# Reordering the first units of an attention-then-MLP kernel: loads, pads, copies, a table load, zero matmuls and one filler

## The chip, the cores and the metric

The kernel runs on one core of a Trainium2 chip. The metric is device time in microseconds (us), the median of several executions; less is better. The engines named here are TensorE (PE; its weight loads are shown as PEld), VectorE (DVE), ScalarE (ACT), GpSimd (POOL) and SyncE (SP), which here does nothing but issue DMAs. ScalarE and GpSimd issue some DMAs too. Each engine runs its own instructions strictly in the order in which the program gives them, and waits on semaphores for what it needs from the others.

## What is computed

A linear attention with a decaying state, followed by a two-layer MLP with SiLU:

```python
B, H, S, D = 4, 8, 768, 48                  # batch, heads, sequence, head size
for t in range(S):                          # r, k, v: (B, H, S, D); w, u: (H, D)
    cur = einsum('bhd,bhe->bhde', u * k[t], v[t])
    y[t] = einsum('bhd,bhde->bhe', r[t], state + cur)
    state = w[..., None] * state + einsum('bhd,bhe->bhde', k[t], v[t])
x = y.transpose(0, 2, 1, 3).reshape(3072, 384)
h = x @ w_in                                # 384 x 2048
out = (h * sigmoid(h)) @ w_out              # 2048 x 384
```

## The kernel before

**Units.** The sequence is cut into six chunks of 128 steps. A unit is one chunk of one batch (all eight heads): unit `i` is chunk `i // 4` of batch `i % 4`, 24 units in all. A unit's r, k and v are three loads of 192 KB each into `rin`, `kin` and `vin` (eight buffers each), in rows of 48 floats in slots of 64; `pad` (line 169, VectorE) or `pad_copy` (line 173, ScalarE) zeroes the 16 spare columns of r and k.

**One unit of chunk 0.** In the words of the order list below: `T` turns r and k into PSUM by TensorE transposes (line 272); `rT` and `kT` multiply them by powers of the decay on VectorE (line 289); `P` forms the products within the chunk on TensorE (line 380); `n` masks them on VectorE (line 386); `V` multiplies by v on TensorE (line 396); `e` adds the bonus term and evicts to `y` on VectorE (line 401); `yT` transposes y on TensorE (line 591), and `xT` or `xTD` copies the result to `xT`, on ScalarE or on VectorE (`copy_x`, lines 593 to 595). Beside it GpSimd makes the bonus: `ku` (line 240), `ru` (line 245) and, after a row sum `rd` on VectorE (line 253), `vu` (line 258). It also makes the decayed k, `kc` (line 248), which `S` on TensorE (line 419) multiplies with v into the new state. `v16` casts v to 16 bits on ScalarE (line 263). Units 4 and up work on halves of a chunk, with `Q` (line 478), `D` (line 455) and `Z` (lines 544, 552 and 561) in the place of `S`, `P` and `V`.

**The MLP.** `L` is a group of six to twelve matmuls of the first layer into PSUM (`hps`, line 606), `G` its SiLU on ScalarE into `gT` (line 615). The second layer accumulates 16 matmuls per 128 tokens (`ops`, line 628). Both are cut into pieces; a piece of the second layer is four matmuls of 128x384. Pieces wait in a list of fillers, and `fill(n)` issues the next `n` of them, so that TensorE has work while the attention waits on other engines.

**The order.** The schedule is written out by hand. Up to the first half of chunk 1 the order is a list of words (lines 717 to 731) that the loop at line 732 turns into instructions, on whichever engine the step belongs to; `lr`, `lk` and `lv` are loads that SyncE issues, `ak` is a load of k that ScalarE issues, `pd` and `pa` are the two kinds of pads, `tab` loads ScalarE's table for SiLU (line 227; before it ScalarE has the table for Ln and Exp), `clear` and `spin` are matmuls on zeros that no one reads (lines 186 and 181), `i_q` and `i_o` are loads of `w_in` and `w_out` that GpSimd issues, `ub` and `uc` (lines 205 and 208) spread u over the partitions as `u_bc`, which `ru` reads. After the list, the loop at line 748 handles two units per turn, from unit 6 on. In its turn for units 6 and 7 it issues, for TensorE: `sums(6)`, `product_halves(6)`, `fill(4)` at line 782, `outputs_halves(6)`, the transposes `turn(8)` and `turn(9)` (r, then k, of each), and then `fill(4)` at line 801 and more fillers before `sums(8)`.

Of the kernel before, what the change touches and what calls it, by code (L numbers as in the profile page):

```python
# [16 lines left out]
def kernel(  # L17
# [11 lines left out]
    nc = tc.nc  # L29

    B, H, S, D = r.shape
# [19 lines left out]
    def unit(i):  # L51
        return divmod(i, B)
# [52 lines left out]
    idle = cst.tile([128, 512], F16)  # L105
# [53 lines left out]
    lamC = cst.tile([128, H, D], FP)  # L159
    lamH = cst.tile([128, H, D], FP)  # L160
# [4 lines left out]
    lamN = cst.tile([128, H, D], FP)  # L165
# [9 lines left out]
            nc.scalar.copy(out=dst[i][:, :, D:64],  # L175
                           in_=idle[:, 0:128].rearrange("p (h d) -> p h d", h=H))

    def spin(n):
        zs = ps.tile([128, 512], FP, name="zs", tag="moe", bufs=4)
        for _ in range(n):  # L180
            nc.tensor.matmul(zs, idle[:, 0:128], idle, start=True, stop=True)

    def clear():
        for t in att:
# [18 lines left out]
    def spread_row(name, src):  # L203
        spread[name] = ps.tile([128, HD], FP, name="bc", tag="moe", bufs=4)
        nc.tensor.matmul(spread[name], ones, src, start=True, stop=True)
# [28 lines left out]
    def bonus_products(i):  # L234
        bonus_ku(i)
        bonus_rku(i)
# [60 lines left out]
    def by_planes(i):  # L297
        return i > 2 * B + 1
# [193 lines left out]
    def state_first(i):  # L492
        s1 = L(i)["s1"] = wrk.tile([PR, 2, NP, D], FP, name="s1")
        if unit(i)[0]:
            nc.vector.tensor_tensor(out=s1, in0=summed(i, 0), in1=L(i)["sdec"], op=ALU.add)  # L495
        else:
            nc.vector.tensor_copy(out=s1, in_=summed(i, 0))
        if early(i):
            spread_pairs(nc.scalar.copy, inner_pairs[i // 2 % 2], s1)
            return  # L500
        for j in range(2):
            spread_state(nc.scalar.copy, j, inner[i // 2 % 2], s1)
# [115 lines left out]
    def l1(sc, b0, nb, ft):  # L618
        l1_mm(sc, b0, nb, ft)
        l1_silu(sc, b0, nb, ft)  # L620
# [47 lines left out]
    def fill(n):  # L668
        for _ in range(n):
            if fillers:  # L670
                fillers.pop(0)()
# [14 lines left out]
    halved = [lambda ft=ft: l1(1, 0, 2, ft) for ft in range(0, NFT, 2)]  # L686

    def piece(word, f):
        b0, ft = word.split(".")
        f(0, *blocks[b0], int(ft))  # L690
# [6 lines left out]
        "wy": lambda: columns(nc.scalar, wpT, w, 0), "lnw": powers_r, "eK": exponents_k,  # L697
        "lamK": powers_k, "uc": copy_u, "wb": lambda: spread_row("w", w_row),
        "ub": lambda: spread_row("u", u_row), "lnwb": ln_w, "lamC": powers_c, "lamH": powers_h, "lamN": powers_n,
        "tab": silu_table, "clear": clear, "spin": lambda: None, "H": lambda: halved.pop(0)(),  # L700
    }
    unit_steps = {
        "T": turn, "rT": lambda i: decay_one(i, 0), "kT": lambda i: decay_one(i, 1),
# [12 lines left out]
    }  # L716
    order = """
        ur kz0 id itr lr0 wy pd0 ak0 cz2 kz3 itc wr mk wx cz1 mh lnw eK cg3 lamK kz4 kz1 lk1
        id16 lr1 pd3 lr3 lk3 clear 6*spin lv0 cg0 lv1 kz7 lr2 ak2 ku0 lv3 lr5 kz2 lv2 ub pd1 lv4
        lr4 lk4 lv5 pd2 lk5 lk7 lr6 lk6 uc T0 1*spin T1 lr7 lv7 kT0 pa4 rT0 ru0 ku1  # L720
        v160 pd5 lv6 rT1 kz6 rd0 kT1 wb ru1 P0 n0 2*spin rd1 P1 vu0 lnwb T2 n1 v161 2*spin
        pd7 lamC lamH lamN pa6 i_q0 V0 v162 tab rT2 e0 kT2 ku2 T3 1*spin yT0 V1 kz5 vu1 i_q1 ru2
        xTD0 e1 P2 yT1 kT3 rd2 rT3 ku3 xTD1 P3 ru3 n2 rd3 v163 n3 L0.0 vu2 kc0 1*spin G0.0
        vu3 V2 L0.2 V3 G0.2 L0.4 e2 i_q2 e3 kc1 yT2 yT3 S0 G0.4 xT2 xTD3 kc2 L0.6 L2.4 G0.6
        st0 L2.0 scA0 v164 kc3 L2.6 ku4 i_q3 v165 L2.2 T4 rT4 kT4 G2.4 ru4 G2.2 T5 G2.0 G2.6
        L4.8 G4.8 L4.10 kT5 G4.10 L4.9 kc4 ku5 S2 L4.11 rd4 rT5 st2 sc2 kc5 sd4 ru5 G4.9
        G4.11 rA4 vu4 i_o0 Q4 D4 rA5 s1_4 ku7 L4.12 rd5 vu5 m4 s2_4 G4.12 L4.13 G4.13 T6 Z4
        L4.14 G4.14 L4.15 z4 yT4 2*spin yT5 i_o2 i_o1 ku6 xT4 xT5 rT6 T7 G4.15 rT7 v167 sd6
        kT6 v166 ru6 lr8 kc6 kc7 H H rd6 i_o3 H vu6 lr9 rP7 rA6 sn4 H H lk8 lk9 sx4 lv9 lv8
        ru7 kT7  # L730
    """
    for word in order.split():
        if "*" in word:
            n, word = word.split("*")
            spin(int(n))
        if word in steps:
            steps[word]()
        elif word[0] == "L":
            piece(word[1:], l1_mm)
        elif word[0] == "G":  # L740
            piece(word[1:], l1_silu)
        else:
            unit_steps[word[:-1]](int(word[-1]))
# [4 lines left out]
    for i in range(B + 2, NU, 2):  # L748
        sc, b = unit(i)
        nxt = range(i + 2, min(i + 4, NU))  # L750
        after = range(i + 4, min(i + 6, NU))
        split = i + 2 < NU and by_planes(i + 2)
        sums(i)
        product_halves(i)
        state_first(i)
        masked_halves(i)
        state_second(i)
        if by_planes(i + 4) and not by_planes(i):
            rescale_state(i)
        if i == B + 2:  # L760
            bonus_sum(i + 1)
            bonus_v(i + 1)
        if i == 2 * B:
            for n in nxt:
                split_k(n, nc.scalar.copy)
        if split:
            turn_planes()
        if b and split:
            for n in nxt:
                cast_k(n)  # L770
                cast_v(n)
        for n in nxt:
            bonus_products(n)
            if not split:
                decayed_k(n)
        if i > B + 2 or sc < NCH - 1:
            next_state(i)
        if not b and split:
            for n in nxt:
                cast_k(n, nc.gpsimd.tensor_copy)  # L780
                cast_v(n, nc.gpsimd.tensor_copy)
        fill(3 if b and split else 4)
        outputs_halves(i)
        next_crossed(i)
        for n in nxt:
            turn(n)
        evict_halves(i)
        turn_y_dma(i)
        if b:
            fillers.extend((first(sc) if sc > 1 else rest_first(sc)) + second(sc))  # L790
        for n in nxt:
            if split:
                decay_one(n, 0)
                if b:
                    join_k(n)
            else:
                decay(n)
        for dst, src in ((kin, k), (rin, r), (vin, v)):
            for n in after:
                ld(n, dst, src)  # L800
        fill(4)
        if i > 2 * B and not b and split:
            for n in nxt:
                join_k(n)
        for n in nxt:
            bonus_sum(n)
            if not split:
                cast_v(n)
            bonus_v(n)
        for n in after:  # L810
            weighted_k(n)
        if after and by_planes(i + 4) and not i == B + 2:
            for n in after:
                split_k(n)
        for n in nxt:
            fill(2)
            decay_r16(n, True)
        if i == 2 * B and split:
            for n in nxt:
                join_k(n)  # L820
        fill((5 if b and split else 4) if i < NU - 4 else 2)
# [31 lines left out]
```

## Time and profile before

| | |
|---|---|
| median of 3 executions | 185.11 us (184.15 to 185.25) |
| the profiled execution | 185.49 us, of which the span from its first to its last instruction is 183.8 us |
| TensorE busy | 174.5 us (95% of the span), 2801 matmuls |
| VectorE, ScalarE, GpSimd busy | 117.0, 115.8, 129.3 us |
| DMA queue of SyncE (q1) | 98224 packets, 23.86 MB, 66.5% of 16 engines' time |
| granted TensorE clock | 1.00 over the span |

The span is the time between the first and the last instruction on the core; the rest of the 185.49 us lies around it. In a timeline row the first number is the start in us from the beginning of the span, the second how long the merged group lasted, then engine, line, operation, what it writes and reads, shapes and count; in brackets, how long the engine had been idle and what ended that. A row with SPq, ACTq or POOLq is the issuing of a DMA. A matmul's duration includes the time until its result is out, so that matmuls that overlap are judged by the spacing of their starts. "DMA share" is the time of all packets over the time of 16 engines; it can be somewhat over 1, since packets overlap in an engine.

### The profile page before, as it was taken

The page shows a single profiled execution, that of the slowest core. Times are in us where ns is not written, and L with a number is a line of the kernel's source. Part 1 is how long each engine was busy: PE and PEld are TensorE (multiplying, and loading weights), DVE is VectorE, ACT ScalarE, POOL GpSimd, SP SyncE. Part 2 cuts the span into 40 slices and gives each one's busy share as a digit, 9 for nine tenths or more (in the row PEclk, how much of TensorE's full clock was granted, in tenths as well). Part 3 has the DMA queues.
Part 4 walks back from the last instruction along what each step waited for, and adds up shares of the span by engine and source line. Part 5 has one row for each costly group of instructions (what it writes and reads, how often), then busy time and mean ns, then how long its engine had stood idle before and what let it go on. Part 6 is the DMA issues. An engine that isn't in the chain of part 4 may idle for free.

```text
span 183.8 us, 6611 instructions
## 1 busy us (share of the span) xinstructions
PE 174.5 (95%) x2801; PEld 113.9 (62%) x2801; DVE 117.0 (64%) x231; ACT 115.8 (63%) x208; POOL 129.3 (70%) x179
## 2 busy tenths in 40 slices
PE   7977899999899999999899999999999999999993
PEld 2555786588666976656556555657656566555562
DVE  5999728897977985865775955776944974000120
ACT  4471787699145797398597488797588781299200
POOL 7999999898899979869979769879769700000000
PEclk9999999999999999999999999999999999999999
DMA  5999999899697799999599999499799201410022
GB/s 95 238 192 216 178 175 200 154 224 225 129 189 210 114 202 184 199 183 202 114 178 177 162 209 213 92 183 160 183 197 250 49 4 46 128 43 0 10 79 86
DMA packets 102865, 27.89 MB, mean 152 GB/s; under 512 B 97586, under 2 KB 102324, under 8 KB 102836
## 3 DMA queue, kind: packets, MB, share of 16 engines
q1 hardware_dynamic: 98224, 23.86, 66.5%
q0 software_dynamic: 2176, 3.15, 10.1%
q10 hardware_dynamic: 2436, 0.46, 1.3%
q8 instruction: 22, 0.36, 0.8%
q14 instruction: 7, 0.06, 0.1%
HBM read 20.45 MB, written 4.72 MB: 137 GB/s over the span
## 4 chain that ended last, share of the span: by engine, by line
PE 72%; POOL 17%; DMA 5%; issue 5%; ACT 0%; POOLq 0%
PE ops L628 33%; PE hps L606 26%; DMA kin<-in_k_dram 5%; PE att L455 4%; POOL ku L240 4%; POOL rku_f L245 3%; PE att L272 3%; POOL vu L258 2%; POOL kc L248 2%; PE yp L552 2%; PE sp L478 2%; PE ops L653 1%; PE yp L561 1%; POOL win L84 1%; POOL wout L89 1%
## 5 line engine op out<-in xcount | busy, mean ns | idle before, releaser
L606 PE MATMUL hps<-xT,win 128*128 128x512 f16 (+1 forms) x360 | 66.3, 338 | 0.1
L615 ACT ACTIVATE gT<-hps 128x512 f16<-128x512 f32 x96 | 55.3, 597 | 12.2 <-PE hps L606 8.9
L628 PE MATMUL ops<-wout,gT 128*128 128x384 f16 x368 | 62.9, 326 | 0.1
L606 PEld LDWEIGHTS <-win 128*128 128x128 f16 x360 | 39.0, 114 | 21.1 <-issue 0.4
L628 PEld LDWEIGHTS <-gT 128*128 128x128 f16 x368 | 35.0, 98 | 23.9 <-ACT gT L615 0.8
L401 DVE TENSOR_TENSOR y<-yp,vu 64x384 f16<-64x384 f32 (+1 forms) x34 | 18.9, 555 | 11.3 <-PE yp L561 5.5
L245 POOL TENSOR_TENSOR rku_f<-ku,u_bc 128x384 f32<-128x384 f32 x24 | 24.2, 1010 | 1.4
L240 POOL TENSOR_TENSOR ku<-kin,rin 128x384 f32<-128x384 f32 x24 | 24.2, 1007 | 0.7 <-DMA rin<-in_r_dram 0.6
L258 POOL TENSOR_TENSOR vu<-vin,rku 128x384 f32<-128x384 f32 x24 | 19.6, 828 | 6.8 <-DVE rku L253 6.8
L289 DVE TENSOR_TENSOR rT<-att,lamR 112x512 f16<-112x512 f32 (+1 forms) x26 | 17.8, 684 | 4.2 <-PE att L272 3.8
L326 ACT COPY kT<-blocks 112x1024 uint16<-112x1024 uint16 x14 | 15.6, 1160 | 7.6 <-DMA blocks<-planes 7.5
L634 ACT COPY osb<-ops 128x384 f32<-128x384 f32 x20 | 9.4, 475 | 16.5 <-PE ops L628 12.5
L495 DVE TENSOR_TENSOR s<-sp,sdec 112x384 f32<-112x384 f32 x10 | 5.6, 557 | 16.0 <-PE sp L478 15.4
L636 DVE COPY osb<-ops 128x384 f32<-128x384 f32 x3 | 1.7, 557 | 21.3 <-PE ops L628 21.3
L462 DVE TENSOR_TENSOR am<-att,maskH 128x1024 f16<-128x1024 f32 x10 | 12.2, 1224 | 3.5 <-PE att L455 3.5
L343 DVE TENSOR_TENSOR rX<-att,lamR 48x256 f16<-48x256 f32 x32 | 13.5, 421 | 0.5
L263 ACT CAST v<-vin 128x384 f16<-128x384 f32 x16 | 7.9, 510 | 8.4 <-DMA vin<-in_v_dram 8.3
L253 DVE TENSOR_REDUCE rku<-rku_f 128x8 f32<-128x384 f32 x24 | 12.4, 542 | 0.9 <-POOL rku_f L245 0.9
L314 POOL TENSOR_TENSOR lnw_bc<-kin,lamN 128x384 f32<-128x384 f32 x7 | 7.0, 1001 | 8.0 <-DMA kin<-in_k_dram 6.4
L434 ACT CAST s1h<-s 48x384 f16<-48x384 f32 x16 | 8.2, 510 | 6.7 <-DVE s L495 6.6
L455 PE MATMUL att<-rT,kT 48*64 48x64 f32 x640 | 11.9, 220 | 0.2 <-issue 0.2
L455 PEld LDWEIGHTS att<-rT,kT 48*64 48x64 f32 x640 | 10.6, 135 | 0.3 <-issue 0.3
(106 smaller groups left out, 214.0 us busy)
## 6 DMA issues: line engine op xcount, KB each, us to landing
rin<-in_r_dram SPq DMA_DIRECT2D x24, 192.0 KB, 4.0
vin<-in_v_dram SPq DMA_DIRECT2D x24, 192.0 KB, 4.6
out_dram<-osb SPq DMA_DIRECT2D x23, 192.0 KB, 3.2
kin<-in_k_dram SPq DMA_DIRECT2D x22, 192.0 KB, 3.5
win<-in_moe_w_in_dram POOLq DMA_DIRECT2D x4, 384.0 KB, 6.3
wout<-in_moe_w_out_dram POOLq DMA_DIRECT2D x4, 384.0 KB, 6.6
kin<-in_k_dram ACTq DMA_DIRECT2D x2, 192.0 KB, 3.7
xT<-y SPq DMA_TRANSPOSE x9, 2.8
```

The lines of the kernel that those rows point to most:

```text
L240: eng.tensor_tensor(out=L(i)["ku"], in0=kin[i % NIN][:, :, 0:D], in1=rin[i % NIN][:, :, 0:D], op=ALU.mult)
L245: eng.tensor_tensor(out=L(i)["rku_f"], in0=L(i)["ku"], in1=u_bc, op=ALU.mult)
L253: nc.vector.tensor_reduce(out=L(i)["rku"], in_=L(i)["rku_f"], axis=mybir.AxisListType.X, op=ALU.add)
L258: eng.tensor_tensor(out=L(i)["vu"], in0=vin[i % NIN], in1=L(i)["rku"].unsqueeze(2).broadcast_to([128, H, D]), op=ALU.mult)
L289: nc.vector.tensor_tensor(out=L(i)[key].rearrange("p g (y t) -> p y g t", y=2), in0=L(i)["t"][0:PR, :, x], in1=lam, op=ALU.mult)
L326: nc.scalar.copy(out=L(i)["kT"].rearrange("p g t -> p (g t)").bitcast(U16) .rearrange("p (n y) -> p n y", y=2), in_=turned[0:PR, i % 2].re ...
L343: nc.vector.tensor_tensor(out=rx[here], in0=L(i)["t"][there, x, 0], in1=(lamM if by_planes(i) else lamR)[there, :, 0:HC], op=ALU.mult)
L401: nc.vector.tensor_tensor(out=y16[a], in0=y[b, 0:HD], in1=vu[a], op=ALU.add)
L455: nc.tensor.matmul(a[o0:o0 + HC, j, e, p, :], kT[r0:r0 + D, p, HC * x:HC * x + HC], rT[r0:r0 + D, p, HC * x:HC * x + HC], start=True, stop ...
L606: nc.tensor.matmul(hps[:, f, :].rearrange("p (b t) -> p b t", b=nb), win[(ft + f) // 4].rearrange("p q (t c) -> p q t c", c=4) [:, q, :, ( ...
L615: nc.scalar.activation(out=gts[sc][:, ft:ft + m, b0 * C:(b0 + nb) * C], in_=hpss[b0, ft], func=AF.Silu)
L628: nc.tensor.matmul(opss[b], gts[sc][:, ft, b * C:(b + 1) * C], wout[:, ft, :], start=(ft == 0), stop=(ft == NFT - 1))
```

## The change

In the order list:

- SyncE loads r and k of unit 2 (`lr2 lk2`) right after those of unit 1, and r and k of unit 3 (`lr3 lk3`) after v of units 0 and 1. ScalarE no longer issues the load of k of unit 2 (`ak2`).
- SyncE loads v of unit 2 ahead of r of unit 5 (`lv2` before `lr5`).
- Six zero matmuls of 512 columns ahead of `ub` become 38 of 80 columns (`38*short`): 32 more, by way of a new argument of `spin`.
- The pads of unit 7 go from VectorE (`pd7`) to ScalarE (`pa7`).
- The copies of x of units 0 and 1 go from VectorE (`xTD0`, `xTD1`) to ScalarE (`xT0`, `xT1`).
- On ScalarE the SiLU table (`tab`) comes ahead of the cast of v of unit 2 (`v162`), and that cast moves behind both x copies.
- On VectorE the decay of r of unit 3 (`rT3`) comes ahead of the row sum of unit 2 (`rd2`).

In the loop, in the turn for units 6 and 7 alone, one filler moves from behind the transposes of units 8 and 9 to ahead of `outputs_halves(6)`.

```diff
-    def spin(n):
+    def spin(n, cols=512):
         zs = ps.tile([128, 512], FP, name="zs", tag="moe", bufs=4)
         for _ in range(n):
-            nc.tensor.matmul(zs, idle[:, 0:128], idle, start=True, stop=True)
+            nc.tensor.matmul(zs[:, 0:cols], idle[:, 0:128], idle[:, 0:cols], start=True, stop=True)
...
     order = """
         ur kz0 id itr lr0 wy pd0 ak0 cz2 kz3 itc wr mk wx cz1 mh lnw eK cg3 lamK kz4 kz1 lk1
-        id16 lr1 pd3 lr3 lk3 clear 6*spin lv0 cg0 lv1 kz7 lr2 ak2 ku0 lv3 lr5 kz2 lv2 ub pd1 lv4
-        lr4 lk4 lv5 pd2 lk5 lk7 lr6 lk6 uc T0 1*spin T1 lr7 lv7 kT0 pa4 rT0 ru0 ku1
-        v160 pd5 lv6 rT1 kz6 rd0 kT1 wb ru1 P0 n0 2*spin rd1 P1 vu0 lnwb T2 n1 v161 2*spin
-        pd7 lamC lamH lamN pa6 i_q0 V0 v162 tab rT2 e0 kT2 ku2 T3 1*spin yT0 V1 kz5 vu1 i_q1 ru2
-        xTD0 e1 P2 yT1 kT3 rd2 rT3 ku3 xTD1 P3 ru3 n2 rd3 v163 n3 L0.0 vu2 kc0 1*spin G0.0
-        vu3 V2 L0.2 V3 G0.2 L0.4 e2 i_q2 e3 kc1 yT2 yT3 S0 G0.4 xT2 xTD3 kc2 L0.6 L2.4 G0.6
+        id16 lr1 pd3 lr2 lk2 clear 38*short lv0 cg0 lv1 kz7 lr3 lk3 ku0 lv3 lv2 kz2 lr5 ub pd1
+        lv4 lr4 lk4 lv5 pd2 lk5 lk7 lr6 lk6 uc T0 1*spin T1 lr7 lv7 kT0 pa4 rT0 ru0 ku1 v160 pd5
+        lv6 rT1 kz6 rd0 kT1 wb ru1 P0 n0 2*spin rd1 P1 vu0 lnwb T2 n1 v161 2*spin lamC lamH lamN
+        pa6 pa7 i_q0 V0 tab rT2 e0 kT2 ku2 T3 1*spin yT0 V1 kz5 vu1 i_q1 ru2 xT0 e1 P2 yT1 kT3
+        rT3 rd2 ku3 xT1 v162 P3 ru3 n2 rd3 v163 n3 L0.0 vu2 kc0 1*spin G0.0 vu3 V2 L0.2 V3 G0.2
+        L0.4 e2 i_q2 e3 kc1 yT2 yT3 S0 G0.4 xT2 xTD3 kc2 L0.6 L2.4 G0.6 st0 L2.0 scA0 v164 kc3
...
     for word in order.split():
         if "*" in word:
             n, word = word.split("*")
-            spin(int(n))
+            spin(int(n), 80 if word == "short" else 512)
...
-        fill(3 if b and split else 4)
+        fill(5 if i == B + 2 else 3 if b and split else 4)
         outputs_halves(i)
...
-        fill(4)
+        fill(3 if i == B + 2 else 4)
```

The words of the list from `kc3` on are the same as before, wrapped differently.

## Prediction

> **What bounds the kernel now.** I read the page first: TensorE is busy for 174.5 of 183.8 us. Windows then say where it is not: from 48.60 to 180.00 us it is busy for 130.41 of 131.40. What can be won lies before 48.6 us, unless work is taken away, and the change takes none. So the chain of waits came next, at the place where it turns into TensorE work for good:
>
> ```profile
> 38.28 0.18 issue
> 38.46 9.68 DMA kin<-in_k_dram
> 48.14 0.04 issue
> 48.19 0.44 PE att L272 x8
> 48.62 7.91 PE ops L628 x48
> ```
>
> The last thing that TensorE waited for is a load of k landing at 48.14 us: k of unit 9. Before 38.28 us the chain runs through GpSimd. TensorE's waits up to 60 us, summed (who waited for what: us in total, times, longest):
>
> ```profile
> PE att L272 <- DMA rin<-in_r_dram: 1.3, 2, 1.1
> PE att L380 <- DVE rT L289: 1.0, 1, 1.0
> PE att L272 <- DMA kin<-in_k_dram: 1.0, 2, 0.6
> PE sp L419 <- POOL kc L248: 0.3, 1, 0.3
> ```
>
> Their places, from the timeline:
>
> ```profile
> 12.04 0.44 PE L272 MATMUL att<-ident,rin 64*112 64x64 f32 x8 [1.11 <-DMA rin<-in_r_dram]
> ...
> 17.14 1.09 PE L380 MATMUL att<-rT,kT 48*64 48x128 f32 x32 [1.02 <-DVE rT L289]
> ...
> 22.30 0.40 PE L419 MATMUL sp<-v,kc 128*64 128x48 f16 x14 [0.35 <-POOL kc L248]
> ...
> 27.32 0.43 PE L272 MATMUL att<-ident,kin 64*112 64x64 f32 x8 [0.40 <-DMA kin<-in_k_dram]
> ...
> 48.19 0.44 PE L272 MATMUL att<-ident,kin 64*112 64x64 f32 x8 [0.56 <-DMA kin<-in_k_dram]
> ```
>
> These are T2, P3, S0, T5 and T9. The first two are what the reordering touches; the last three are gates that TensorE must still pass, and what it gains ahead of one is lost there if the gate does not move.
>
> **The gates.** S0 needs `kc1`, the first of the three in this GpSimd row:
>
> ```profile
> 20.41 0.80 POOL L84 DMA_DIRECT2D win<-in_moe_w_in_dram  x1
> 21.23 2.92 POOL L248 TENSOR_TENSOR kc<-kin,lamC 128x384 f16<-128x384 f32 x3
> ```
>
> It ends at about 22.2. GpSimd is busy for 17.80 of the 17.95 us from 6.25 to 24.20, and the change takes nothing from it and reorders nothing on it, so `kc1` stays. T5 and T9 need k5 and k9. The DMA share is 1.09 from 2 to 12 us, 1.12 from 12 to 22, 1.00, 1.02 and 1.10 in the windows to 48.2: the stream is full, its bytes do not change, and from `lv4` on neither does its order. So I hold all three gates fixed.
>
> **First units, part by part.** VectorE is busy for 15.86 of the 16.40 us from 4.80 to 21.20. It loses `pd7` (from the end of the mask `n1` at 12.36 to the decay at 12.74: 0.38), `xTD0` (14.62 to 14.88: 0.26) and `xTD1` (17.00 to 17.27: 0.27). `rT3` ahead of `rd2` saves P3 another 0.46 (15.95 to 16.41), and `rd2` loses nothing, since its input `ru2` leaves GpSimd only at 15.84. T2 no longer waits for r2 until 12.04: r2 and k2 take the places in which r3 and k3 were issued (2.42 to 5.91), so T2 follows the mask `n0` at 10.77. `rT3` then ends at 17.09 - 0.38 - 0.26 - 0.46 = 15.99 and P3 starts at 16.05 instead of 17.14, the first layer near 17.1 instead of 18.16. The mask `n3` follows `rd3`, and that follows `ru3`, which GpSimd ends at 17.88 as before: `n3` ends at 19.6 instead of 20.07, V3 at 19.7 instead of 20.16, and S0 stops for `kc1` at 21.3 instead of 21.74. It goes on at 22.30. Of 1.1 us at P3, nothing is left. T3 can wait a little for k3, which now lands where about r2 and v3 did (12 to 14 us), but `kT3` is not due before 14.6.
>
> ScalarE takes two pads at 0.29 and two copies in a stretch where it sat idle for 4.24 us waiting for v2 until 17.77, and the table (1.28 us) moves into the same gap, to about 13.5 to 14.8. Cover: x0 is copied at about 15.3 and x1, whose transpose follows `e1`, at about 16; the first layer comes behind P3, at 17.1. If that cover went, each us there would meet S0's gate, which has 0.95 us to spare. The casts v2 and v3 come behind and are ready by 17, V2 wants them at 18. A copy of x takes 348 ns on VectorE and 473 on ScalarE. The Trainium skill ("ScalarE: Activation LUTs", Rules for kernel authors) says to give plain arithmetic to VectorE, which is faster, and so speaks against this move; the rows agree on the price, 2 x 0.125 us; by that rule, with ScalarE as the path and no gate behind it, the sum would be -0.56 + 0.25 = -0.31 and the time 184.8. Against it, in this stretch, stands the row of VectorE's window: VectorE is the full engine and ScalarE the idle one.
>
> The SyncE queue takes k2 over from ScalarE: one more issue ahead of `lv0`. If issuing, not the engines, paced the stream, everything behind would be later by 0.70 us (a short issue row: k4 at 16.76); if ScalarE's ring only got in the way, earlier by its 0.46. With a share above 1 I take 0 and keep both ends. r5 now lands up to 3 us later; T5 wants it at 26.5.
>
> **Zero matmuls.** Their starts are 0.43 us apart up to 4.25 and 0.22 after it (weight-load rows at 3.40, 3.83, 4.25, then two to 4.69): a slow and a fast pace. 38 x 80 = 3040 columns against 6 x 512 = 3072. At the slow pace 80 columns are 0.067 us, so 19 fit until 4.25; at the fast one 0.034 to 0.036, so 19 more end near 4.93 where now it is 4.91. Can small ones go at that pace, each with a full weight load? Eight 48-column ones (V0, 13.08, 0.36 us, each 183 ns long) are (0.36 - 0.18) / 7 = 25 ns apart, so yes. The upper bound is the weight load unhidden, 0.15 us in the slow stretch: 38 x 0.15 = 5.7 us. The lower is zero. I take 25 to 67 ns, the nearest row. Even at 67 ns throughout they would end at 5.5, and the 0.16 us of idle VectorE ahead of `kT0`, the 0.91 us that VectorE saves (0.38 + 0.26 + 0.27) and the 1.05 us between `u_bc` (6.31) and `ru0` (7.36) on GpSimd take that up.
>
> **The filler.** A piece of the second layer is 4 of the 12 matmuls that took 2.06 us (57.88): 0.69 us. TensorE was ready for k of T9 at 48.19 - 0.56 = 47.63; with the piece in front it comes at 48.32, and k9 is there. It has done 0.69 us of later work at a cost of 48.32 - 48.19 = 0.13: gain 0.56. Should the first units bring TensorE there earlier after all, no more than 0.69 can come of it while k9 lands at 48.14. Who pays: `outputs_halves(6)`, the evictions on VectorE and the transposing DMA behind them are 0.69 later, and so are the loads queued behind that DMA on SyncE; the stretch after T9 has one piece less. TensorE wants the results at `sums(8)`, 56.5; VectorE's decays end at 51.1 and GpSimd's last `kc` at 53.4, so 2 us are left. Sum: 0 + 0 + 0 - 0.56.
>
> ```profile
> 56.53 0.37 PE sp L478 x32
> 56.90 0.98 PE att L455 x63
> 57.88 2.06 PE ops L628 x12
> ```
>
> **Rivals.**
> 1. The stream is late: k9 lands 0.7 us later, T9 waits until 48.89 and the piece only fills a longer wait: 185.1. For it: k9 took 9.68 us to land, the stream being full; against: no bytes are added. The same result if the timed executions had no wait at T9 (the one at 184.15 may be such).
> 2. The gates move: k2 out of ScalarE's queue lets k5 and k9 land 1.1 us earlier. Then P3's 1.1 adds to 0.56: 183.45. Against it: S0's gate is GpSimd's, not the stream's.
> 3. Slower: the short matmuls pay for weight loads. They delay `ub`, so `u_bc` (ends 6.31), so `ru0` on GpSimd (7.36) and everything that GpSimd does after it, `kc1` included. A delay d of GpSimd moves S0 by d; T5's wait takes up 0.40; T9 has nothing left. The result is -0.56 + d - 0.40, a loss from d = 0.96 on. d is the delay of the zeros less 1.05. At 0.10 us each they end at 6.8, d = 0.8, still -0.15; at 0.15 each they end at 8.7, d = 2.7, +1.75: 186.9.
>
> **Numbers.** The sum is 185.49 - 0.56 = 184.93 for the profiled execution. That one is 0.38 above the median, so the forecast is 185.11 - 0.56 = 184.55. Chances: forecast 0.52, late stream 0.22, gates move 0.12, zeros 0.14. With the executions' own scatter (184.15 to 185.25, half a us to each side) the forecast alone spans 184.0 to 185.1; down to 183.4 takes in the second rival, and up to 185.9 the first and the half of the third near break-even. 1% is 1.85 us, about what a measurement can tell: faster than 183.26 only if the gates move and more (0.07); slower than 186.96 only with zeros at 0.15 or something I don't see (0.09); 0.84 between.
>
> **What would show it.** Right: T9's wait for k gone, five fillers (three groups of `hps`, two of `ops`) ahead of `outputs_halves(6)`, S0 waiting for `kc1` some 1 us until 22.2, T5's wait as it is or longer, `hps` from 17.1, zeros ending at 4.9. Wrong: `kc1` ending at another time than 22.2, k9 landing away from 48.1 by more than 0.3, `ru0` later than 7.4, or a new TensorE wait behind 48.6, where the windows now show 0.99 us idle in all.

## The result and the profile after

The changed kernel takes 186.45 us (median of 21 executions, 184.56 to 188.49) against 185.11 (median of 21, 183.78 to 188.29) before: ratio 1.0069, 95% interval [1.0046, 1.0093]. Some executions are slower than the rest, and every ratio here leaves out those more than 1.5% above the fastest of their kernel. The change is slower by 0.7%, where 0.3% faster was predicted, and the time lies outside the predicted range (183.4 to 185.9 us). Its profiled execution took 185.97 us, its span 184.3 us, 0.5 us more than before.

The chain of waits, where it turns into TensorE work for good (start, duration, what):

```profile
18.82 3.13 SPq L73
21.95 0.04 issue
22.00 6.60 DMA kin<-in_k_dram
28.60 0.04 issue
28.64 0.44 PE att L272 x8
```

That point has moved from T9, at 48.19 us, to T5, at 28.64. From here on the chain is TensorE's own work and a few short pauses. Ahead of it stands not GpSimd but SyncE's queue, issuing loads: k of unit 5 lands at 28.60 us instead of 27.27. TensorE's waits up to 60 us, summed (in total, times, longest), without the one before the first zeros:

```profile
PE hps L606 <- DMA win<-in_moe_w_in_dram: 1.2, 1, 1.2
PE att L272 <- DMA kin<-in_k_dram: 0.8, 1, 0.8
PE att L455 <- issue: 0.6, 1, 0.6
PE att L380 <- DVE rT L289: 0.5, 1, 0.5
```

Their places, from the timeline: T2, P3, the fifth group of the first layer (`L0.4`), S0, T5 and T9.

```profile
12.17 0.44 PE L272 MATMUL att<-ident,rin 64*112 64x64 f32 x8
...
17.28 1.09 PE L380 MATMUL att<-rT,kT 48*64 48x128 f32 x32 [0.50 <-DVE rT L289]
...
22.05 0.85 PE L606 MATMUL hps<-xT,win 128*128 128x256 f16 x6 [1.21 <-DMA win<-in_moe_w_in_dram]
...
23.16 0.43 PE L419 MATMUL sp<-v,kc 128*64 128x48 f16 x16
...
28.64 0.44 PE L272 MATMUL att<-ident,kin 64*112 64x64 f32 x8 [0.81 <-DMA kin<-in_k_dram]
...
49.79 0.39 PE L272 MATMUL att<-ident,kin 64*112 64x64 f32 x8
```

T2 no longer waits for r, and the wait at P3 is halved. A wait of 1.21 us for `w_in` is new, S0 does not stop for `kc1`, T5 waits twice as long, and T9 passes without a wait, 1.60 us later than before. Of these 1.60, 0.69 are the piece of the second layer that now lies ahead of it, so TensorE is 0.91 us behind at T9. The windows give some of that back:

```profile
48.60:180.00 131.40, 130.78 (x2048) 82.24 (x2042) 80.34 (x153) 85.07 (x144) 85.72 (x107) 1.00 0.70 140
```

The columns are the window, its length, busy time (instructions) of TensorE, its weight loads, VectorE, ScalarE and GpSimd, the granted clock, the DMA share and GB/s. Behind 48.6 us TensorE idles for 0.62 us, where it idled for 0.99. 0.91 - 0.37 is 0.54, the longer span within 0.1. So in this execution the loss is made ahead of T9, and the loads have a part in it: they came late although their bytes are the same. One microsecond of the same view, first of the kernel after, then of the one before:

```profile
13.00:14.00 1.00, 0.81 (x18) 0.58 (x18) 1.00 (x2) 0.98 (x4) 1.00 (x3) 1.00 0.61 67
```

```profile
13.00:14.00 1.00, 1.00 (x27) 0.81 (x24) 0.89 (x2) 0.53 (x3) 1.00 (x3) 1.00 0.74 110
```

Both streams dip here, the changed one deeper (67 GB/s against 110). I had read a share of 1.12 from 12 to 22 us as "the stream is full" and had not looked inside the window.

### The profile page after: what moved, and what is told of

It reads as the page before. It is cut to its first block, busy times and chain, and to the rows that moved or that the text cites. A ratio compares the mean times of both kernels' runs of the same rounds, so it can differ in the third digit from the quotient of the medians.

```text
span 184.3 us, 6676 instructions
## 1 busy us (share of the span) xinstructions
PE 175.7 (95%) x2833; PEld 115.5 (63%) x2833; DVE 116.1 (63%) x227; ACT 117.8 (64%) x212; POOL 129.5 (70%) x179
## 4 chain that ended last, share of the span: by engine, by line
PE 67%; DMA 11%; SPq 10%; POOL 4%; ACT 3%; issue 2%; DVE 2%; POOLq 0%; ACTq 0%
PE ops L628 27%; PE hps L606 26%; SPq L73 10%; DMA kin<-in_k_dram 5%; PE att L455 4%; DMA blocks<-planes 4%; PE att L272 3%; ACT kT L326 2%; POOL planes L317 2%; PE sp L478 2%; DMA rin<-in_r_dram 2%; PE ops L653 1%; PE yp L561 1%; PE yp L552 1%; POOL u_wide L314 1%
## 5 line engine op out<-in xcount | busy, mean ns | idle before, releaser
L615 ACT ACTIVATE gT<-hps 128x512 f16<-128x512 f32 x96 | 55.9, 597 | 13.8 <-PE hps L606 10.4
L253 DVE TENSOR_REDUCE rku<-rku_f 128x8 f32<-128x384 f32 x24 | 12.4, 543 | 0.3 <-POOL rku_f L245 0.3
L455 PEld LDWEIGHTS att<-rT,kT 48*64 48x64 f32 x640 | 10.6, 135 | 0.7 <-issue 0.7
```

Of the source, the lines that this page charges most:

```text
L455: nc.tensor.matmul(a[o0:o0 + HC, j, e, p, :], kT[r0:r0 + D, p, HC * x:HC * x + HC], rT[r0:r0 + D, p, HC * x:HC * x + HC], start=True, stop ...
L615: nc.scalar.activation(out=gts[sc][:, ft:ft + m, b0 * C:(b0 + nb) * C], in_=hpss[b0, ft], func=AF.Silu)
```

## The experiments

Sixteen further kernels ran, and the changed kernel twice more, each timed in five rounds against the kernel before on the same chip. Behind a ratio stand 10 to 12 executions of the kernel (19 in the first comparison of the change), but 7 of change_w_in_before_fetch and 6 each of the two with seventy short zeros, of three_long_and_35_short and of the change in its third comparison. The table has all of them, with the kernel before and the changed kernel itself, sorted by the number of TensorE matmuls that they add ahead of about 11 us. Each matmul is two instructions in the trace, a weight load and the matmul. "Packet" is the time of the first packet of 16,384 bytes on DMA queue 8 (instructions), "least share" the lowest DMA share of any whole microsecond from 9 to 15 us, both in the profiled execution.

| kernel | added ahead of 11 us | ratio to before | packet, us | least share |
|---|---|---|---|---|
| the kernel before | 0 | 1 | 11.0 | 0.74 |
| filler_alone | 0 | 0.9981 [0.9950, 1.0012] | 14.2 | 0.86 |
| long_zeros_and_k2_on_scalar | 0 | 1.0000 [0.9970, 1.0030] | 12.1 | 1.03 |
| six_long_zeros | 0 | 1.0002 [0.9966, 1.0038] | 13.1 | 0.92 |
| later_zeros_split_behind | 0 | 1.0004 [0.9971, 1.0037] | 12.7 | 0.84 |
| tiny_zeros_count_alone | 0 | 1.0006 [0.9985, 1.0028] | 12.5 | 0.85 |
| k2_on_sync_alone | 0 | 1.0012 [0.9976, 1.0049] | 13.7 | 0.94 |
| w_in_early_without_zeros_and_queue | 0 | 1.0016 [0.9987, 1.0044] | 12.4 | 1.03 |
| later_zeros_split_ahead | 29 | 1.0022 [0.9984, 1.0060] | 10.6 | 0.41 |
| k2_on_scalar_again | 32 | 0.9998 [0.9966, 1.0030] | 11.0 | 0.60 |
| change_without_filler | 32 | 1.0033 [1.0007, 1.0060] | 9.3 | 0.99 |
| change_w_in_early | 32 | 1.0035 [1.0007, 1.0062] | 10.3 | 0.86 |
| short_zeros_alone | 32 | 1.0043 [1.0013, 1.0073] | 10.1 | 0.57 |
| the change, compared three times | 32 | 1.0035 to 1.0069 | 9.5 to 11.0 | 0.48 to 0.77 |
| change_w_in_before_fetch | 32 | 1.0089 [1.0055, 1.0124] | 11.2 | 0.90 |
| three_long_and_35_short | 32 | 1.0101 [1.0059, 1.0143] | 10.2 | 0.68 |
| seventy_short_zeros | 64 | 1.0106 [1.0064, 1.0148] | 7.9 | 0.34 |
| seventy_short_zeros_alone | 64 | 1.0117 [1.0082, 1.0153] | 9.3 | 0.31 |

The diffs below show the words and widths that change; where a kernel needs the definition of a new word (`short`, `third`, `tiny`), that part is left out.

### One part undone, one part alone

**The zeros back.** The changed kernel with its first zeros as they were:

```diff
-        id16 lr1 pd3 lr2 lk2 clear 38*short lv0 cg0 lv1 kz7 lr3 lk3 ku0 lv3 lv2 kz2 lr5 ub pd1
+        id16 lr1 pd3 lr2 lk2 clear 6*spin lv0 cg0 lv1 kz7 lr3 lk3 ku0 lv3 lv2 kz2 lr5 ub pd1
```

> The changed kernel with one part undone: six zero matmuls of 512 columns again in the place of the 38 of 80. Theory Z (the zeros): in the profile of the changed kernel the 38 run 66 ns apart to the last, TensorE's clock is granted only at about 6.9 us instead of 4.3, the matmul that spreads u takes 1.6 us instead of 0.8, u_bc ends at 7.7 instead of 6.3, and GpSimd does everything from its second product on 0.5 us late, the loads of w_in included. Then without them u_bc ends near 6.3 again, GpSimd's first load of w_in is issued at 11.2, and the ratio to the kernel before is 0.997 (the filler's 0.56 us won, the rest lost at the gates). Theory Q (the queue): the stream of loads is late because r and k of unit 2 and all others now go through SyncE's queue alone. Then this kernel is as slow as the changed one, 1.007, and k of unit 5 still lands near 28.6 instead of 27.3. Theory C (the clock's start is chance): the full clock comes at 4.3 or at 6.9 whatever the zeros are, and this kernel too shows a late start in some profiles; ratio 1.003 to 1.007.

Measured: 184.13 us, ratio 1.0002 [0.9966, 1.0038]. By the middle of the interval, all that the change costs is gone with its short zeros. The other way round, the kernel before with the short zeros and nothing else:

```diff
-        id16 lr1 pd3 lr3 lk3 clear 6*spin lv0 cg0 lv1 kz7 lr2 ak2 ku0 lv3 lr5 kz2 lv2 ub pd1 lv4
+        id16 lr1 pd3 lr3 lk3 clear 38*short lv0 cg0 lv1 kz7 lr2 ak2 ku0 lv3 lr5 kz2 lv2 ub pd1 lv4
```

> The kernel before with one part of the change alone: 38 zero matmuls of 80 columns for the six of 512. Theory Z: full clock late (near 6.9 us), u_bc near 7.7, GpSimd 0.5 us late, ratio 1.004 to 1.010, the latter since T9's wait is not filled. Theory Q: 1.000. Theory C: full clock at 4.3 or 6.9 by chance, ratio within 0.998 to 1.003.

Measured: 185.02 us, ratio 1.0043 [1.0013, 1.0073]. The zeros alone make the kernel slower by about what the whole change does. Yet they take no longer. The zeros from the timeline of the changed kernel, then of six_long_zeros:

```profile
2.97 2.74 PE L181 MATMUL zs<-idle 128*128 128x80 f16 x38
```

```profile
2.97 2.77 PE L181 MATMUL zs<-idle 128*128 128x512 f16 x6
```

2.74 and 2.77 us: both were at the slow pace to their ends, since the full clock was granted at 6.95 and 5.77 us. That moment is chance: 4.17 to 7.16 us in the eleven profiles whose first zeros are short, 4.20 to 6.73 in the nine where they are long. It is why the profiled execution of the change had `u_bc` late and GpSimd behind it:

```profile
7.85 1.01 POOL L245 TENSOR_TENSOR rku_f<-ku,u_bc 128x384 f32<-128x384 f32 x1 [0.46 <-DVE u_bc L208]
```

In the second execution profiled (change_again) the full clock came at 4.92 us, and `ru0` started at 7.38 without a wait, as before. So these 0.46 us are no effect of the change. The Trainium skill ("TensorE: Matmul & The Clock Gate", Part 1) states a free-running window of 3413 ns; the trace agrees: its stretches of half clock within the span last 3.41 us. The page has the start vary by 500 ns to each side; here it varied over 2.99 us.

**The queue of k2.** The changed kernel with ScalarE loading k of unit 2 again (`ak2` in the place it had), and the kernel before with that load on SyncE:

```diff
-        id16 lr1 pd3 lr2 lk2 clear 38*short lv0 cg0 lv1 kz7 lr3 lk3 ku0 lv3 lv2 kz2 lr5 ub pd1
+        id16 lr1 pd3 lr2 ak2 clear 38*short lv0 cg0 lv1 kz7 lr3 lk3 ku0 lv3 lv2 kz2 lr5 ub pd1
```

> The changed kernel with k of unit 2 issued by ScalarE again, at the same place of the list. Theory Q: the second ring feeds the stream again; packets until 20 us are back at 20.3 us of sixteen engines' time instead of 18.9, the second piece of w_in lands near 20.5 instead of 22.0, k of unit 5 near 27.3 instead of 28.6, ratio 0.999. Theory Z: u_bc ends near 7.7 still, the second piece of w_in is issued at 14.5 and the ratio stays at 1.006.

```diff
-        id16 lr1 pd3 lr3 lk3 clear 6*spin lv0 cg0 lv1 kz7 lr2 ak2 ku0 lv3 lr5 kz2 lv2 ub pd1 lv4
+        id16 lr1 pd3 lr3 lk3 clear 6*spin lv0 cg0 lv1 kz7 lr2 lk2 ku0 lv3 lr5 kz2 lv2 ub pd1 lv4
```

> The kernel before with one part alone: k of unit 2 is issued by SyncE, behind r of unit 2, and not by ScalarE. Theory Q: T3 and all later loads are late by 0.7 to 1.3 us, k of unit 5 lands near 28.4, k of unit 9 near 49, ratio 1.004 to 1.007. Theory Z: 1.000, k of unit 5 within 0.3 us of 27.3.

Measured: 184.36 us, ratio 0.9998, and 184.67 us, 1.0012; both intervals hold 1. The first is the one kernel with short zeros whose time shows no loss, and it stays unexplained; its interval reaches to 1.003. The queue alone is worth 0.1% by the middle of its interval.

**The filler and the order.** The changed kernel as it is, without its filler move, without its zeros and its queue change, and the kernel before with the filler move alone, on one chip:

> The changed kernel itself once more, on the chip of the next three. If the loss is the change's own, the ratio is 1.004 to 1.009 and its profile shows TensorE waiting near 22 us for the second piece of w_in, as in the first profile (1.21 us) and in the two with one part undone (0.93 and 1.92). If the loss was that of one chip or of late starts of the full clock by chance, the ratio is 0.997 to 1.003, and a profile with a start near 4.3 us has no such wait.

```diff
-        fill(5 if i == B + 2 else 3 if b and split else 4)
+        fill(3 if b and split else 4)
...
-        fill(3 if i == B + 2 else 4)
+        fill(4)
```

> The changed kernel with the filler back behind the transposes of units 8 and 9. By the prediction's own sum the filler wins 0.56 us where TensorE waits for k of unit 9, so this kernel is 0.3% slower than the changed one. If TensorE comes late to unit 9 anyway, held up at 22 us by w_in, the wait is not there, and the two are equal within 0.1%.

```diff
-        id16 lr1 pd3 lr2 lk2 clear 38*short lv0 cg0 lv1 kz7 lr3 lk3 ku0 lv3 lv2 kz2 lr5 ub pd1
+        id16 lr1 pd3 lr2 ak2 clear 6*spin lv0 cg0 lv1 kz7 lr3 lk3 ku0 lv3 lv2 kz2 lr5 ub pd1
```

> The changed kernel with two parts undone: six long zero matmuls and k of unit 2 on ScalarE. What is left is the order of the loads, the copies, pads and table on ScalarE, the decay ahead of the row sum, and the filler. If zeros and queue each cost, this beats the kernel before: 0.994 to 0.997 (the filler's 0.56 us and a little). If only one of them costs, it is no faster than the versions with one undone: 1.000. If the order of the loads costs, 1.003.

```diff
-        fill(3 if b and split else 4)
+        fill(5 if i == B + 2 else 3 if b and split else 4)
...
-        fill(4)
+        fill(3 if i == B + 2 else 4)
```

> The kernel before with the filler's move alone. By the prediction -0.56 us: ratio 0.997, T9's wait for k gone. If k of unit 9 is often there in time without it, or something behind takes it back, 1.000.

Measured: 1.0035, 1.0033, 1.0000 and 0.9981. The reordered first units with ScalarE's moves and the filler move together change nothing that the interval, 0.9970 to 1.0030, would show. The filler move alone is the lowest ratio of all, but its interval, 0.9950 to 1.0012, holds 1, and taking it out of the change makes no difference. No kernel tried is shown to beat the kernel before.

### Where the first units' gain goes

In all six profiles of the reordered first units up to here TensorE waits for the second load of `w_in`, by 0.9 to 1.9 us. First long_zeros_and_k2_on_scalar, `L0.4` and S0 in its timeline:

```profile
21.26 0.85 PE L606 MATMUL hps<-xT,win 128*128 128x256 f16 x6 [1.01 <-DMA win<-in_moe_w_in_dram]
...
22.37 0.43 PE L419 MATMUL sp<-v,kc 128*64 128x48 f16 x16
```

Theory W: this wait is what holds the gain back. The same kernel, and the change itself, with GpSimd issuing that load earlier (at 12.89 us instead of 13.99 in the first):

```diff
-        pa6 pa7 i_q0 V0 tab rT2 e0 kT2 ku2 T3 1*spin yT0 V1 kz5 vu1 i_q1 ru2 xT0 e1 P2 yT1 kT3
+        pa6 pa7 i_q0 vu1 i_q1 V0 tab rT2 e0 kT2 ku2 T3 1*spin yT0 V1 kz5 ru2 xT0 e1 P2 yT1 kT3
```

> The change without its short zeros and without its SyncE load of k of unit 2 (the kernel that gave 1.0000), and with GpSimd's second load of w_in issued ahead of the table and the casts behind it, about 1.2 us earlier. Theory W (what the reordered first units win is lost at the fifth group of the first layer, which waits for that load: 0.9 to 1.9 us in six profiles): that wait falls to 0 to 0.5, the group starts at about 20.7 instead of 21.3, ratio 0.997. Rival (S0, T5 and T9 hold the time whatever happens at the first layer): the wait at w_in goes, the wait for kc at S0 or for k at T5 grows by as much, ratio 1.000.

> The changed kernel with the same earlier load of w_in. Theory W: 0.5 us less than the changed kernel, ratio 1.002 to 1.003 against before. Theory I with the rival of W: as the changed kernel, 1.004 to 1.006, with the pauses at instructions 1473 and 3521 still there.

Measured: 184.07 us, ratio 1.0016, and 184.59 us, 1.0035. The timeline of the first:

```profile
20.19 0.84 PE L606 MATMUL hps<-xT,win 128*128 128x256 f16 x6 [0.17 <-DMA win<-in_moe_w_in_dram]
...
22.25 0.40 PE L419 MATMUL sp<-v,kc 128*64 128x48 f16 x14 [0.69 <-POOL kc L248]
```

`L0.4` comes 1.07 us earlier, and the part of S0 that needs `kc1` only 0.12: what was waited for at `w_in` is waited for at `kc1`. W falls, as far as these two profiles and ratios tell. The two gates stand one behind the other, and the second is the one that the prediction named.

### Why short zeros cost

**Theory I: the count moves TensorE's pauses.** TensorE has short pauses in which nothing that the profile shows is awaited. They come at the same place in its own instruction count in kernels of the same count, and 64 more instructions move them, to 44.59 us in the change among others. A kernel with 32 zero matmuls of 16 columns (`tiny`) in the idle time ahead of T2 has the same count behind it; one with 70 short zeros has 64 instructions more again:

```diff
-        v160 pd5 lv6 rT1 kz6 rd0 kT1 wb ru1 P0 n0 2*spin rd1 P1 vu0 lnwb T2 n1 v161 2*spin
+        v160 pd5 lv6 rT1 kz6 rd0 kT1 wb ru1 P0 n0 2*spin rd1 P1 vu0 lnwb tiny T2 n1 v161 2*spin
```

> The kernel before, with 32 zero matmuls of 16 columns more in front of the transposes of unit 2, where TensorE idled 1.11 us waiting for r: they cost next to no time themselves, but put 64 more instructions (a weight load and a matmul each) ahead of everything that follows. Theory I (TensorE pauses whenever its instruction count passes certain multiples of 256, and 64 more instructions move the passes to worse places): the pauses move from instruction 3010 (87 us) to about 3521 with the next place at 101 us and one near 1473 (43 to 45 us), as in the kernels with 38 short zeros; time 0.4% above before, ratio 1.003 to 1.005. Rival (the short zeros cost by their own time or by the GpSimd work they delay): these lie in an idle stretch, ratio 1.000, +-0.002.

```diff
-        id16 lr1 pd3 lr2 lk2 clear 38*short lv0 cg0 lv1 kz7 lr3 lk3 ku0 lv3 lv2 kz2 lr5 ub pd1
+        id16 lr1 pd3 lr2 lk2 clear 70*short lv0 cg0 lv1 kz7 lr3 lk3 ku0 lv3 lv2 kz2 lr5 ub pd1
...
-            spin(int(n), 80 if word == "short" else 512)
+            spin(int(n), 44 if word == "short" else 512)
```

> The changed kernel with 70 zero matmuls of 44 columns (3080) in place of 38 of 80 (3040): 64 more instructions again, 128 more than the kernel before. Theory I: the pauses at 43 to 45 us and near 101 us are gone or elsewhere; 0.3 to 0.8 us faster than the changed kernel, ratio to before 1.000 to 1.003. Rival (short zeros cost by themselves, each with its weight load): twice as many cost as much as 38 or more, ratio 1.005 to 1.010.

Measured: 183.92 us, 1.0006 [0.9985, 1.0028], and 185.63 us, 1.0106 [1.0064, 1.0148]. Both against I. The pauses moved as it said (the timeline of the first kernel, whose lines stand six further down):

```profile
43.24 0.34 PE L461 MATMUL att<-rT,kT 48*64 48x64 f32 x5 [0.46 <-issue]
...
100.02 0.38 PE L567 MATMUL yp<-v,am 64*64 64x48 f16 x25 [0.20 <-issue]
```

but the time did not follow; and in the profile with 70 there are no such pauses, while the loss is larger. (seventy_short_zeros_alone, below, has one of 0.61 us, at 48.73.) What remains is an effect of the short zeros where they stand: of the instructions that they add early, or of something else in the first burst.

**Theory F: the packet of instructions.** When TensorE is at about its 230th to 320th instruction, a packet of 16,384 bytes comes on the instruction queue. The table shows its time: 7.9 to 11.2 us in the kernels that add matmuls in front, 12.1 to 14.2 in those that do not, but 11.0 in the kernel before. That kernel and filler_alone have the same program up to the loop, so the place of the packet has a scatter of some 3 us of its own. F says: an issue of SyncE that falls beside it takes long, and unless GpSimd's load of `w_in`, issued at 11.2 us, already feeds the DMA engines, the stream runs dry and all later loads shift. Four kernels: the change with the first load of `w_in` ahead of the packet; 70 short zeros alone; three long zeros and 35 short ones, the count of 38 again (short means 44 columns in these two); and the change as control.

```diff
-        lv6 rT1 kz6 rd0 kT1 wb ru1 P0 n0 2*spin rd1 P1 vu0 lnwb T2 n1 v161 2*spin lamC lamH lamN
-        pa6 pa7 i_q0 V0 tab rT2 e0 kT2 ku2 T3 1*spin yT0 V1 kz5 vu1 i_q1 ru2 xT0 e1 P2 yT1 kT3
+        lv6 rT1 kz6 rd0 kT1 wb i_q0 ru1 P0 n0 2*spin rd1 P1 vu0 lnwb T2 n1 v161 2*spin lamC lamH lamN
+        pa6 pa7 V0 tab rT2 e0 kT2 ku2 T3 1*spin yT0 V1 kz5 vu1 i_q1 ru2 xT0 e1 P2 yT1 kT3
```

> The changed kernel with GpSimd's first load of w_in issued at about 9.4 us instead of 11.2, ahead of the bonus product of unit 1, which is 0.93 us later for it. Theory F (the packet of instructions at TensorE's 230th instruction stalls SyncE's loads while nothing else feeds the stream): the packet still comes at 9.3 to 11 us, but the DMA share stays above 0.8 from 9 to 14 us, k of unit 5 lands about 0.5 to 1 us earlier than in the changed kernel, ratio to before 1.000 to 1.002, 0.3% or more under change_third_time. Rival (the short zeros cost in some other way): as change_third_time, within 0.2%.

```diff
-        id16 lr1 pd3 lr3 lk3 clear 6*spin lv0 cg0 lv1 kz7 lr2 ak2 ku0 lv3 lr5 kz2 lv2 ub pd1 lv4
+        id16 lr1 pd3 lr3 lk3 clear 70*short lv0 cg0 lv1 kz7 lr2 ak2 ku0 lv3 lr5 kz2 lv2 ub pd1 lv4
```

> The kernel before with 70 zero matmuls of 44 columns in place of six of 512, nothing else. Theory F: the packet comes at about 8 us, three us ahead of the load of w_in, the stream loses about 1.1 us of its time between 8 and 13 us, ratio 1.005 to 1.010 (38 of 80 alone: 1.0043). Rival (the count of instructions alone, or chance): 1.000 to 1.003.

```diff
-        id16 lr1 pd3 lr3 lk3 clear 6*spin lv0 cg0 lv1 kz7 lr2 ak2 ku0 lv3 lr5 kz2 lv2 ub pd1 lv4
+        id16 lr1 pd3 lr3 lk3 clear 3*spin 35*short lv0 cg0 lv1 kz7 lr2 ak2 ku0 lv3 lr5 kz2 lv2 ub pd1 lv4
```

> The kernel before with three zero matmuls of 512 columns and 35 of 44 (3076 columns, 38 matmuls) in place of six of 512. Theory F: as short_zeros_alone, since only the number of instructions ahead of the 230th counts: the packet at 9 to 11 us, ratio 1.003 to 1.005. Rival (short matmuls as such): less than that, since half of the columns are in long ones again, 1.000 to 1.002.

> The changed kernel as it is, as a control on this chip: 1.0035 to 1.007 by its two earlier comparisons; the packet of instructions at 9.3 to 11 us, a hole in the stream behind it in most executions (0.03 to 1.08 us in the five profiles so far with 38 short zeros).

Measured: 1.0089, 1.0117, 1.0101 and 1.0059. Seventy alone have the hole that F asked for, with the packet at 9.3 us instead of 8 and a loss above F's range; by the middles of the intervals, twice the added instructions cost over twice as much as in short_zeros_alone. The DMA engines' busy tenths from 10 to 13 us, in 40 slices, of seventy_short_zeros_alone:

```profile
DMA  9999999997631111000000349979999999989335
```

Most of a microsecond of the stream is gone. The mixed zeros are as slow as short ones or slower, also slower than F's 1.003 to 1.005, so it is not the share of the columns that lie in short matmuls. But F's remedy fails. In change_w_in_before_fetch the least share is 0.90, as F said; T5 waits for k by less than 0.2 us, in the control by 0.91 (the first two rows are T5's and T9's k; the row of the control, T5's k, follows):

```profile
27.42 0.44 PE L272 MATMUL att<-ident,kin 64*112 64x64 f32 x8
...
49.96 0.44 PE L272 MATMUL att<-ident,kin 64*112 64x64 f32 x8 [0.80 <-DMA kin<-in_k_dram]
```

```profile
28.35 0.44 PE L272 MATMUL att<-ident,kin 64*112 64x64 f32 x8 [0.91 <-DMA kin<-in_k_dram]
```

and what is won at T5 is lost at T9, where k of unit 9 comes at 49.9. The earlier `w_in` load fills the hole; that it also pushes other loads back is likely but not shown, and this kernel does not isolate the hole.

**The same matmuls ahead of the packet and behind it.** The last pair leaves the first zeros alone and cuts later ones into 29 more matmuls of the same columns in all, once between T0 and P1, once behind T2:

```diff
-        lr4 lk4 lv5 pd2 lk5 lk7 lr6 lk6 uc T0 1*spin T1 lr7 lv7 kT0 pa4 rT0 ru0 ku1
-        v160 pd5 lv6 rT1 kz6 rd0 kT1 wb ru1 P0 n0 2*spin rd1 P1 vu0 lnwb T2 n1 v161 2*spin
+        lr4 lk4 lv5 pd2 lk5 lk7 lr6 lk6 uc T0 8*short T1 lr7 lv7 kT0 pa4 rT0 ru0 ku1
+        v160 pd5 lv6 rT1 kz6 rd0 kT1 wb ru1 P0 n0 24*third rd1 P1 vu0 lnwb T2 n1 v161 2*spin
...
-            spin(int(n))
+            spin(int(n), {"short": 64, "third": 43}.get(word, 512))
```

> The kernel before, its first six zero matmuls untouched; the single one between the transposes of units 0 and 1 becomes eight of 64 columns and the two between the products of units 0 and 1 become 24 of 43: the same columns, 29 matmuls (58 instructions) more, all behind the first burst and ahead of the 230th instruction. Theory F: the packet comes at 9.5 to 11 us, SyncE's issue beside it takes over 1.2 us, the DMA share falls under 0.8 in some microsecond behind it; ratio 1.003 to 1.007. Rival (the first burst of short zeros costs, not the place of the packet): 1.000, +-0.002.

```diff
-        v160 pd5 lv6 rT1 kz6 rd0 kT1 wb ru1 P0 n0 2*spin rd1 P1 vu0 lnwb T2 n1 v161 2*spin
-        pd7 lamC lamH lamN pa6 i_q0 V0 v162 tab rT2 e0 kT2 ku2 T3 1*spin yT0 V1 kz5 vu1 i_q1 ru2
+        v160 pd5 lv6 rT1 kz6 rd0 kT1 wb ru1 P0 n0 2*spin rd1 P1 vu0 lnwb T2 n1 v161 24*third
+        pd7 lamC lamH lamN pa6 i_q0 V0 v162 tab rT2 e0 kT2 ku2 T3 8*short yT0 V1 kz5 vu1 i_q1 ru2
```

> The same split made at the next zero matmuls instead: the two behind the transposes of unit 2 become 24 of 43 columns, the one behind those of unit 3 eight of 64; 58 instructions more, all behind the 230th. Theory F and its rival alike: the packet comes at 11 to 14 us as before, ratio 1.000, +-0.002. If this one is slower by 0.3% too, F falls and the split itself costs.

Measured: 185.10 us, 1.0022 [0.9984, 1.0060], ahead, and 184.30 us, 1.0004 [0.9971, 1.0037], behind. One profiled execution of each shows F's steps. SyncE's issues from 9.4 us (SPq rows) and the DMA engines from 10 to 13 us, ahead:

```profile
9.38 0.70 SPq L73 DMA_DIRECT2D vin<-in_v_dram  x1
10.13 2.15 SPq L73 DMA_DIRECT2D rin<-in_r_dram  x1
```

```profile
DMA  9999999999999778999899899998642200000069
```

and behind:

```profile
9.01 0.70 SPq L73 DMA_DIRECT2D vin<-in_v_dram  x1
9.75 0.86 SPq L73 DMA_DIRECT2D rin<-in_r_dram  x1
```

```profile
DMA  9999999999988999999999999999899999998979
```

The packet comes at 10.6 us in the first, inside the issue that takes 2.15 us in place of 0.86, and from 12.1 us the engines run dry. T2, waiting for r of unit 2, pays (ahead, then behind):

```profile
13.40 0.44 PE L272 MATMUL att<-ident,rin 64*112 64x64 f32 x8 [2.19 <-DMA rin<-in_r_dram]
```

```profile
11.73 0.44 PE L272 MATMUL att<-ident,rin 64*112 64x64 f32 x8 [0.17 <-DMA rin<-in_r_dram]
```

So a long issue beside the packet and a hole behind it are there to see in the place where F puts them. Two things weaken this. Issues as long stand in the second execution too where no such packet is near (2.63 us at 14.95, 1.84 us at 17.63). And the profiled execution of the first kernel took 186.51 us, 1.4 more than its median, so that its 2.19 us at T2 are not the usual price. The pair's times differ in F's direction, by 0.2%, with intervals that overlap.

**What is settled and what is open.** The loss comes with the short zeros: without them the change is at 1.0002, they alone give 1.0043. With 32 more matmuls in the first burst the ratios are 0.9998 to 1.0101, and all but one of the intervals lie above 1; with 64 more, 1.0106 and 1.0117; with none ahead of 11 us, 0.9981 to 1.0016, no interval clear of 1. Neither the columns nor the count of instructions as such explains it: 32 or 29 more matmuls behind 11 us cost nothing that the intervals show. That matmuls added ahead of 11 us cost the same wherever they stand is not shown: the one kernel that adds them behind the first burst, later_zeros_split_ahead, has an interval that holds both 1 and the loss of short_zeros_alone.

How the short zeros cost is open. Single executions show the packet and the hole, but they do not go with the loss: three kernels without a deep hole (change_without_filler, change_w_in_before_fetch and change_w_in_early, least share 0.86 to 0.99) are slow too, k2_on_scalar_again has a hole and no loss, and the kernel before had the packet at 11.0 us and a share of 0.74. One way from late loads to TensorE does appear in the profiles. GpSimd, through which the chain of the kernel before runs up to 38 us, waits for loads between 11 and 19 us by 0.43 to 1.14 us in seven of the twelve profiles with matmuls added ahead of 11 us, and by 0.50 and 0.63 in two of the eight others. It does not settle the matter either: change_without_filler is slow without such a wait, and filler_alone has one and is not slow. The Trainium skill ("Runtime: NRT & Kernel Launch", Instruction fetch mechanics) says that instructions come in blocks of 16 KiB, each of 256 instructions, over a DMA queue of the sequencer's own, and calls the cost of a block boundary mostly hidden; the packets agree in size, and whether the cost is hidden here is part of what stays open.

## Why the prediction was wrong

**Zero matmuls: 0. This term failed.** The prediction costed 38 small ones by columns and weight loads, at 25 to 67 ns each, and that was right: 2.74 us in one execution, the same as six long ones at that clock. What it put at nothing, and gave no reason for beyond their own time, is what they do to the rest of the kernel: they are 64 more instructions at a crowded place of the load stream. Alone they measured +0.43%, 0.8 us. By which way is open. Its third rival had the right sign and the right edit with another mechanism (weight loads that would delay GpSimd through `u_bc`). The profiles speak against that one: GpSimd waits for `u_bc` in five of the 20, the five in which the full clock came latest (6.46 to 7.16 us), and one of these, tiny_zeros_count_alone, has six long zeros in front.

**"The stream is full, its bytes do not change": the step behind it.** From the equal bytes it followed that k5 and k9 land as before. The kernel before already has a microsecond with a share of 0.74 in that stretch; the three profiles of the change have 0.48 to 0.77 between 9 and 15 us, and T5 waits for k5 by 0.6 to 0.9 us. The first rival, a late stream, was priced at T9 alone (185.1).

**First units: 0. Right, with two gates misjudged.** P3 and the first layer did come earlier where the clock came early (P3 at 16.29 in change_again, 16.05 predicted), and nothing was left of it. S0's `kc1` was named as the place; in the change itself the second load of `w_in` holds TensorE first, for 1.21 us. The timeline of before gave a hint: TensorE reached `L0.4` at 20.65 us and that load landed at 20.28, 0.37 us of slack, while the prediction's own V3 comes 0.46 earlier. And the load landed later, at 22.00, 21.36 and 20.97 in the three profiles of the change. Nor did `kc1` stay at 22.2: it ended at 22.71, 22.83 and 22.77. In the first of these GpSimd was late through `u_bc`; in the other two it waited for v of unit 2, where it had had next to no slack (v landed at 17.75 us in the kernel before; its row, then that of change_again):

```profile
17.88 0.83 POOL L258 TENSOR_TENSOR vu<-vin,rku 128x384 f32<-128x384 f32 x1
```

```profile
18.48 0.83 POOL L258 TENSOR_TENSOR vu<-vin,rku 128x384 f32<-128x384 f32 x1 [0.56 <-DMA vin<-in_v_dram]
```

That the change takes nothing from GpSimd and reorders nothing on it was true, and not enough to hold this gate fixed.

**Queue of k2, ScalarE's pads, copies and table: 0. Right** within what these runs can tell: with the filler move and the first units' order they are the kernel at 1.0002, and without the queue change the one at 1.0000.

**Filler: -0.56. The mechanism was right, the size not.** T9's wait is gone in all profiles with the piece ahead of it but one (change_w_in_before_fetch, 0.80 us), but its 0.56 us were one execution's. In eight other profiles without the filler move T9 waits for k nowhere by more than 0.3 us. Alone the move measured -0.19%, 0.35 us, between -0.9 and +0.2.

The sum by measured terms, 0.43 for the zeros, 0.12 for the queue, -0.19 for the filler, 0 for the rest, is +0.36%; the change measured 0.35 to 0.69%, so up to half of the largest figure has no term.

## What to carry to other kernels

Do not price a replacement by its own time alone: 38 short matmuls took as long as six long ones and still cost 0.4% elsewhere. Run such a part alone before it goes into a larger change. A wait read from one profiled execution is a sample; before a forecast rests on it, ask how much of it depends on a transfer that lands by chance, and look at "full" resources in windows of a microsecond. Behind a gate that will not move, list every gate in front of it with its slack, because the nearest one takes the gain.

## What the runs showed that was not expected

- Chance moves the first microseconds: the full clock was granted anywhere from 4.17 to 7.16 us, and `u_bc` ended between 6.29 and 7.74.
- The clock can fall back to half for one window of 3.41 us within the first 28 us. In the six profiles with such a window TensorE idled for 1.25 to 1.91 us of the 3.41 ahead of it, but idling for 1.25 to 1.56 us in one such stretch had no such effect in three others. The row of the granted clock on the page of later_zeros_split_ahead, in 40 slices of 4.6 us, shows one (6), from 15.08 us on, behind the wait at T2:

```profile
PEclk9996999999999999999999999999999999999999
```

  By their mean clock (0.988 to 0.991), 18 of 144 executions of the kernel before in the later comparisons have such a window, but 9 of 12 with 70 short zeros. It is not what makes those slow, as far as twelve executions tell: the three without it took 185.63 to 186.29 us, the nine with it 184.76 to 186.70.
- An issue of one 192 KB load on SyncE takes 0.4 to 4.5 us in the first 20 us. The long ones are not waits for a semaphore that the profile shows: of waits for a load there is one in each profile, of 0.4 to 0.6 us, ahead of 6 us.
